# Opening of a fused FNet and gated-SwiGLU kernel: first x block in halves, high parts first, some splits and gate sums moved into later items

## The chip, the cores and the metric

The kernel runs on one core of one Trainium2 chip. The metric is device time in microseconds of one execution, median of several runs. A core has TensorE for matrix products, VectorE, ScalarE and GpSimd for elementwise work, SyncE (SP), and 16 DMA engines; each engine works through its own instruction stream in order, and streams wait for each other by semaphores.

## The reference

With x of 2048 x 512, fp32, the output is `g * a + (1 - g) * b`:

```
g = sigmoid((x * gate_w).sum(-1, keepdims=True))
a = re(DFT_seq) @ (x @ re(DFT_hid).T) - im(DFT_seq) @ (x @ im(DFT_hid).T)
b = (silu(x @ w1) * (x @ w3)) @ w2        # w1, w3: 512 x 1376, w2: 1376 x 512
```

The Fourier matrices come as inputs. All products are fp32.

## The kernel before, in words

**High and low parts.** An fp32 product is made from three products of a reduced type: high x high, high x low, low x high. `split` makes the parts: `high` (L108) is a ScalarE copy that rounds, `low` (L111) a VectorE subtraction of source and high part. `mm3` (L119) issues the three products of 128x128 weights with 512 columns.

**Strassen-Winograd.** Each large product is cut into 2 x 2 blocks and done with seven block products instead of eight. Of x there are the blocks B11, B12, B21, B22 and the differences T1 = B12 - B11, T2 = B22 - T1, T3 = B22 - B12 and T4 = B21 - T2; every one of the seven that are used (`OPS`) is split into the tile `xo`. Of a weight chunk (128 columns of w1 and of w3) three raw blocks, split into `wa` (places 0, 1 and 2, the last is A22), and four sums `wu` (L248 to L251), split into `wb`, are used. Weights arrive raw in `ws` tiles, four buffers in turn, so a load of chunk w + 4 waits until everything has read chunk w.

**The first stage.** The work on w1 and w3 goes in items, one per weight chunk and half of x (chunk 0 to 8 with half 0 first). Item 0 is done plainly, with eight block products (`plain`), because its forms are ready first: C00, C10, C01 and C11, each from two block products. Items 1 to 3 have their first two products, X (`first1`) and Y (`first2`), ahead of time. ScalarE copies X into `s1`; VectorE adds Y to it, the gate sum (L293); `gate1` is the Silu of that (L297). Before the items, this opening is ordered by a scheduler of the tile framework; from item 1 on the order is as written.

**An item**, `gate_up(n)`: X gets two sums' product (wb 1 with T2) and is copied (L356); then the list `early`; then the bank Z is begun (wb 2 with T3) and copied by ScalarE into `u4` (L359); then the sums of the next weights, the first product X of item n + 3 and the high part of the next wb; X gets wb 0 with T1 and VectorE adds it to `u4` (L367); the low part of the next wb; then the list `mid`; Z goes on accumulating in its bank with A22 and T4, and VectorE adds it and multiplies by the gate (L372, L373); the next-but-three weights are split; Y of item n + 3 and its gate sum; last, X gets wb 3 with B22, a Silu (L384) and a product (L388). Functions that are put into `early`, `mid` and `at_end` for an item run at these places; they fetch and split the second half of x, fetch and store other weights.

**Loads.** All loads are issued by SP in order, at first: the first block of chunk 0, B11, the other three blocks of chunk 0, B21, B12, chunk 1, B22, chunks 2 to 4. `load_xo` issues a block of x. Eleven small warm-up products (L398) run on TensorE until B11 is there. Stores of `wb` (L263) and of results (L322) are issued by GpSimd.

The later stages (Fourier products in blocks, w2, the output) are not touched by the change.

Of the kernel before, what the change touches and what calls it, by code (L numbers as in the profile page):

```python
# [7 lines left out]
F32 = mybir.dt.float32  # L8
# [4 lines left out]
P = 128  # L13
# [19 lines left out]
def fnet_swiglu_gate_kernel(  # L33
# [20 lines left out]
    nc = tc.nc  # L54

    def pool(name, bufs, side, space=None):
        kw = {} if space is None else {"space": space}
        cm = tc.tile_pool(name=name, bufs=bufs, side=side, reuse_waits="tile", **kw)
        return cm, cm.__enter__()
# [11 lines left out]
    wu_cm, wup = pool("wu", 1, "right")  # L71
# [8 lines left out]
    def bank(k, name):  # L80
        return psum.tile([P, 512], F32, tag=f"ps{k}", name=name)
# [14 lines left out]
    def wide(name):  # L96
        return take(F4, [P, 1024], F32, name)
# [4 lines left out]
    def free(*tiles):  # L102
        for t in tiles:
            _, places, at = HELD.pop(id(t))
            places.append(at)

    def high(hi, src):
        nc.scalar.activation(hi, src, AF.Copy)  # L108

    def low(hi, lo, src):  # L110
        nc.vector.tensor_sub(lo, src, hi.bitcast(F32))  # L111

    def split(hi, lo, src):
        high(hi, src)
        low(hi, lo, src)

    def mm3(ps, ah, al, bh, bl, first, last, chain=False):
        for n, (u, v) in enumerate(((ah, bh), (ah, bl), (al, bh))):
            nc.tensor.matmul(ps, u, v, start=first and n == 0, stop=last and n == 2,  # L119
                             skip_group_check=chain)  # L120
# [13 lines left out]
    def flat(ap):  # L134
        return ap.rearrange("p a n -> p (a n)")
# [53 lines left out]
    XO, ST = {}, {}  # L189
    XRAW = ("B12", "B11", "B21", "B22")  # L190

    def flat_x(ap):
        return ap.rearrange("p q n -> p (q n)")

    def load_xo(g, k):

        if g not in XO:
            XO[g] = (xo1 if g else xo0).tile([P, 2, 7, 2, 512], F32R, tag="xo", name=f"xo{g}")
        ST[g, k] = wide(f"xs{g}_{k}")
        nc.sync.dma_start(ST[g, k], xt[g, XRAW.index(k)])  # L200

    OPS = ("B11", "B21", "B22", "T1", "T2", "T3", "T4")
    SUMS = {"T1": ("B12", "B11"), "T2": ("B22", "T1"), "T3": ("B22", "B12"), "T4": ("B21", "T2")}
# [5 lines left out]
    def xo_parts(g, k):  # L209
        o = XO[g][:, :, OPS.index(k)]  # L210
        return flat_x(o[:, 0]), flat_x(o[:, 1]), ST[g, k]

    def split_xo(g, k):
        split(*xo_parts(g, k))

    WS, WA, WB = {}, {}, {}

    def back(w):
        return w >= NC and SETS[w] > 0
# [13 lines left out]
    def wa_parts(w, lo, hi):  # L233
        return (*(flat(WA[w][:, h, lo:hi]) for h in range(2)), flat(WS[w][:, lo:hi]))

    def prep_wa(w, lo=0, hi=3):

        if lo == 0:
            WA[w] = wap.tile([P, 2, 3, 256], F32R, tag="wa", name=f"wa{w}")
        split(*wa_parts(w, lo, hi))  # L240

    WU = {}

    def sums_wb(w):

        r = WS.pop(w)
        u = WU[w] = wup.tile([P, 4, 256], F32, tag="wu", name=f"wu{w}")
        nc.vector.tensor_add(u[:, 0], r[:, 3], r[:, 2])  # L248
        nc.vector.tensor_sub(u[:, 1], u[:, 0], r[:, 0])
        nc.vector.tensor_sub(u[:, 2], r[:, 0], r[:, 3])  # L250
        nc.vector.tensor_sub(u[:, 3], r[:, 1], u[:, 1])  # L251

    def wb_parts(w):
        return flat(WB[w][:, 0]), flat(WB[w][:, 1]), flat(WU[w])
# [15 lines left out]
    def prod(ps, n, wi, xi, start, chain=False):  # L270
        w = WSET[n]
        w, wi = (WA[w], wi) if wi < 3 else (WB[w], wi - 3)
        x = XO[ITEMS[n][1]]
        for q in range(2):
            sl = slice(q * P, (q + 1) * P)
            mm3(ps, w[:, 0, wi, sl], w[:, 1, wi, sl], x[:, 0, xi, q, :], x[:, 1, xi, q, :],
                start and q == 0, q == 1, chain)
# [9 lines left out]

    def first2(n):

        y = bank(4 + n % 2, f"Y{n}")  # L290
        prod(y, n, 1, 1, True)
        s1 = G[n][1]
        nc.vector.tensor_add(s1, s1, y)  # L293
        put_score(n, 0, s1)

    def gate1(n):
        nc.scalar.activation(G[n][1], G[n][1], AF.Silu)  # L297
# [28 lines left out]
    early, mid, at_end = {}, {}, {}  # L326
# [5 lines left out]
    def gate_up(n):  # L332
        last = NI - 1
        x, s1 = G.pop(n)
        z = bank(6 + n % 2, f"Z{n}")
        if n == last - 1:

            u2, g1 = (s1p.tile([P, 512], F32, tag="s1", name=f"{k}_{n}") for k in ("u2", "g1"))
        else:
            h = hp.tile([P, 1024], F32, tag="h", name=f"h{n}")  # L340
            u2, g1 = h[:, :512], h[:, 512:]
        u4 = u4p.tile([P, 512], F32, tag="u4", name=f"u4_{n}")
        nw = WSET[n + 1] if n < last else 0
        if nw in WB or nw == 0:
            nw = None
        elif back(nw):
            load_wb(nw)
            nw = None
        wa = WSET[n + LOOK + 1] if n + LOOK < last else 0
        if wa in WA or wa == 0:  # L350
            wa = None
        else:
            load_w(wa, 0, 3 if back(wa) else 4)

        prod(x, n, 4, 4, False, True)
        nc.scalar.activation(u2, x, AF.Copy)  # L356
        run(early, n)
        prod(z, n, 5, 5, True, True)
        nc.scalar.activation(u4, z, AF.Copy)  # L359
        if nw is not None:  # L360
            sums_wb(nw)
        if n + LOOK <= last:
            first1(n + LOOK)
        if nw is not None:
            high_wb(nw)
        prod(x, n, 3, 3, False, True)
        nc.vector.tensor_add(u4, u4, x)  # L367
        if nw is not None:
            low_wb(nw)
        run(mid, n)  # L370
        prod(z, n, 2, 6, False, True)
        nc.vector.tensor_add(u2, u2, z)  # L372
        nc.vector.tensor_mul(u2, s1, u2)  # L373
        store_h(n, 0, u2)
        if wa is not None:
            WA[wa] = wap.tile([P, 2, 3, 256], F32R, tag="wa", name=f"wa{wa}")
            parts_a = wa_parts(wa, 0, 3)
            high(parts_a[0], parts_a[2])
        if n + LOOK <= last:
            first2(n + LOOK)  # L380
        if wa is not None:
            low(*parts_a)
        prod(x, n, 6, 2, False, True)
        nc.scalar.activation(g1, x, AF.Silu)  # L384
        put_score(n, 1, x)
        if n + LOOK <= last:
            gate1(n + LOOK)
        nc.vector.tensor_mul(g1, g1, u4)  # L388
        store_h(n, 1, g1)
        run(at_end, n)  # L390
# [10 lines left out]
    def plain(b12, a21):  # L401

        c = {}

        def half(i, j, w, x, start):
            if start:
                c[i, j] = bank((0, 4, 6, 7)[2 * i + j], f"C{i}{j}")
            for r in range(2):
                sl = slice(r * P, (r + 1) * P)
                mm3(c[i, j], w(0, sl), w(1, sl), x(r, 0), x(r, 1), start and r == 0,  # L410
                    not start and r == 1)

        def wa(k):
            return lambda h, sl: WA[0][:, h, k, sl]

        def xb(k):
            return lambda q, h: XO[0][:, h, k, q, :]

        w21 = lambda h, sl: a21[:, h, sl]
        x12 = lambda q, h: b12[:, h, q * 512 : (q + 1) * 512]  # L420
        s1 = s1p.tile([P, 512], F32, tag="s1", name="s1_0")
        g1 = u4p.tile([P, 512], F32, tag="u4", name="g1_0")
        h = hp.tile([P, 1024], F32, tag="h", name="h0")
        yield half(0, 0, wa(0), xb(0), True)
        yield half(1, 0, w21, xb(0), True)
        half(0, 0, wa(1), xb(1), False)
        nc.scalar.activation(s1, c[0, 0], AF.Silu)
        yield half(1, 0, wa(2), xb(1), False)
        nc.vector.tensor_mul(h[:, :512], s1, c[1, 0])
        store_h(0, 0, h[:, :512])  # L430
        half(0, 1, wa(0), x12, True)
        yield half(1, 1, w21, x12, True)
        half(0, 1, wa(1), xb(2), False)
        nc.scalar.activation(g1, c[0, 1], AF.Silu)
        half(1, 1, wa(2), xb(2), False)
        nc.vector.tensor_mul(h[:, 512:], g1, c[1, 1])
        yield store_h(0, 1, h[:, 512:])
# [31 lines left out]
    gate1(1)  # L469
    sum_xo(0, "T1", hp.tile([P, 1024], F32, tag="h", name="t1"))  # L470
    sum_xo(0, "T2", ST[0, "B11"])
    prep_wa(2)
    first1(2)
    first2(2)
    gate1(2)
    split_xo(0, "T2")
    prep_wb(1)
    sum_xo(0, "T3", ST[0, "B12"])
    split_xo(0, "T3")
    prep_wa(3)  # L480
    first1(3)
    first2(3)
    gate1(3)
    split_xo(0, "T1")
    prep_wa(4)
    sum_xo(0, "T4", ST[0, "B21"])
    split_xo(0, "T4")
    free(*(ST[0, b] for b in ("B11", "B21", "B12", "B22")))

    def do(work, n, f, *a):  # L490
        work.setdefault(n, []).append(lambda: f(*a))


    for k in ("B11", "B21", "B12", "B22"):
# [79 lines left out]
    n = NI - 1 - LOOK  # L574
# [335 lines left out]
    for i, (src, sp, p) in enumerate(late):  # L910
        blk, b = 1 + i // 2, i % 2
        n = (17, 24)[b]
# [11 lines left out]
    for p in range(KD):  # L924
        early = p < NG - NP2
# [71 lines left out]
```

## Time and profile before

| | |
|---|---|
| median of 3 runs | 712.57 us (712.29 to 712.75) |
| profiled execution | 712.41 us, span 710.6 us |
| TensorE, VectorE, ScalarE busy | 99%, 85%, 52% of the span |
| products of the first kernel item start | 5.63 us |
| from 15 us to 30 us | TensorE and VectorE both busy 4.98 to 5.00 of each 5 us |

A row of a timeline holds its start and length in us, the engine, the line, the operation, the tiles written and read, shapes and count; in brackets the idle time before it and who ended it. Equal instructions that follow each other are merged. A product shows a length of some 0.39 us, but the next starts 0.23 us after it: the products overlap. Tile names stand without their numbers: `C` is a bank of item 0, `X`, `Y`, `Z` those of the later items, `s` the gate sums and their Silu, `u` the tile `u4` and `h` the results.

### The profile page before, as it was taken

The numbers are of one execution on the slowest core, as the hardware profiler recorded it, in microseconds if no ns is written. First come the engines' busy times: TensorE is split into PE (matmuls) and PEld (weight loads), VectorE is DVE, ScalarE is ACT, GpSimd is POOL, SyncE is SP. The second block draws the span as 40 slices with busy tenths as digits, with TensorE's granted clock in tenths as the row PEclk, the third lists the DMA queues.
The fourth block names the chain that finished last, engine by engine and source line by source line (L and its number), as shares of the span: only waits on it lengthen the run. The fifth ranks groups of instructions, "written<-read, shape, count | busy, mean of one in ns | idle before, by whom it ended". The sixth has DMA issues, their size and how long they took to land.

```text
span 710.6 us, 8590 instructions
## 1 busy us (share of the span) xinstructions
PE 704.8 (99%) x3089; PEld 578.7 (81%) x3089; DVE 602.4 (85%) x731; ACT 369.0 (52%) x477; POOL 65.7 (9%) x120
## 2 busy tenths in 40 slices
PE   9999999999999999999999999999999999999997
PEld 5888888888888887888888888888888888888886
DVE  6979988787679989886999599969997896898985
ACT  6665555655445755454554553544445355445451
POOL 0011111121110000000110001100110000000000
PEclk9999999999999999999999999999999999999999
DMA  7585546489997496712496228915999971773932
GB/s 280 190 300 209 211 191 254 183 308 353 420 413 267 159 323 226 302 60 89 159 350 276 89 99 318 367 40 199 371 419 416 362 264 63 296 278 140 322 119 89
DMA packets 45691, 173.59 MB, mean 244 GB/s; under 512 B 5328, under 2 KB 5456, under 8 KB 41808
## 3 DMA queue, kind: packets, MB, share of 16 engines
q1 hardware_dynamic: 32464, 118.50, 45.2%
q0 software_dynamic: 12896, 54.02, 19.7%
q8 instruction: 24, 0.39, 0.2%
q10 hardware_dynamic: 288, 0.52, 0.2%
q14 instruction: 19, 0.16, 0.1%
HBM read 115.87 MB, written 57.16 MB: 243 GB/s over the span
## 4 chain that ended last, share of the span: by engine, by line
PE 90%; DVE 4%; DMA 3%; ACT 1%; issue 1%; SPq 0%; POOL 0%; ACTq 0%; DVEq 0%; POOLq 0%
PE P L119 61%; PE X L119 16%; PE Z L119 8%; PE Y L119 4%; DVE zo L111 2%; DMA B<-cc 1%; PE C L119 1%; DVE B L653 1%; DMA xs_B<-xt 1%; ACT zo L108 1%; DMA gate<-gsp 0%; DVE a L111 0%; ACT L730 0%; DVE xo L111 0%; DVE B L656 0%
## 5 line engine op out<-in xcount | busy, mean ns | idle before, releaser
L119 PE MATMUL P<-zo,a 128*128 128x512 f32 x1344 | 306.0, 390 | 0.5 <-DVE zo L111 0.5
L119 PEld LDWEIGHTS P<-zo,a 128*128 128x128 f32 x1344 | 251.8, 188 | 54.5 <-DVE zo L111 2.4
L108 ACT ACTIVATE zo<-B 128x1024 fp32r<-128x1024 f32 (+1 forms) x182 | 189.1, 1045 | 186.2 <-PE P L119 95.9
L111 DVE TENSOR_TENSOR zo<-B,zo 128x1024 fp32r<-128x1024 f32 (+1 forms) x182 | 218.0, 1206 | 50.0 <-ACT zo L108 49.2
L119 PE MATMUL P<-zo,H 128*128 128x512 f32 x468 | 106.2, 389 | 0.0
L119 PEld LDWEIGHTS P<-zo,H 128*128 128x128 f32 x468 | 87.8, 188 | 18.2
L653 DVE TENSOR_TENSOR B<-B,B 128x1024 f32<-128x1024 f32 (+1 forms) x78 | 93.2, 1195 | 0.1
L119 PE MATMUL X<-xo,wb 128*128 128x512 f32 x378 | 92.7, 389 | 0.0
L119 PEld LDWEIGHTS X<-xo,wb 128*128 128x128 f32 x378 | 70.9, 188 | 14.7
L119 PE MATMUL P<-zo,Y 128*128 128x512 f32 x336 | 76.3, 389 | 0.0
L119 PEld LDWEIGHTS P<-zo,Y 128*128 128x128 f32 x336 | 63.1, 188 | 13.1
L322 POOL DMA_DIRECT2D hsp<-h x42 | 23.0, 548 | 127.0 <-DVE h L373 75.5
L119 PE MATMUL X<-xo,wa 128*128 128x512 f32 x126 | 32.3, 389 | 0.0
L119 PE MATMUL Z<-xo,wa 128*128 128x512 f32 x126 | 32.3, 390 | 0.0
L119 PE MATMUL Y<-xo,wa 128*128 128x512 f32 x126 | 32.1, 389 | 0.0
L119 PE MATMUL Z<-xo,wb 128*128 128x512 f32 x126 | 32.1, 389 | 0.0
L870 ACT ACTIVATE zu<-P 128x512 f32<-128x512 f32 x32 | 19.0, 597 | 20.3 <-PE P L119 20.3
L367 DVE TENSOR_TENSOR u<-u,X 128x512 f32<-128x512 f32 x21 | 14.4, 687 | 17.6 <-PE X L119 15.3
L656 DVE TENSOR_TENSOR B<-B,B 128x1024 f32<-128x1024 f32 x24 | 29.3, 1219 | 0.0
L119 PEld LDWEIGHTS Z<-xo,wa 128*128 128x128 f32 x126 | 23.6, 188 | 5.3 <-DVE xo L111 0.4
L119 PEld LDWEIGHTS Y<-xo,wa 128*128 128x128 f32 x126 | 23.6, 188 | 4.9
L119 PEld LDWEIGHTS X<-xo,wa 128*128 128x128 f32 x126 | 23.6, 188 | 4.9
(134 smaller groups left out, 553.8 us busy)
## 6 DMA issues: line engine op xcount, KB each, us to landing
B<-cc SPq DMA_DIRECT2D x64, 512.0 KB, 6.7
hsp<-h POOLq DMA_DIRECT2D x42, 256.0 KB, 3.7
B<-hsp SPq DMA_DIRECT2D x20, 512.0 KB, 10.4
wbsp<-wb POOLq DMA_DIRECT2D x8, 1024.0 KB, 4.2
wb<-wbsp SPq DMA_DIRECT2D x8, 1024.0 KB, 7.8
B<-zsp SPq DMA_DIRECT2D x16, 512.0 KB, 8.2
H<-w2sp SPq DMA_DIRECT2D x6, 1024.0 KB, 8.9
ws<-w SPq DMA_DIRECT2D x11, 512.0 KB, 6.9
```

What stands on the lines that cost most here:

```text
L108: nc.scalar.activation(hi, src, AF.Copy)
L111: nc.vector.tensor_sub(lo, src, hi.bitcast(F32))
L119: nc.tensor.matmul(ps, u, v, start=first and n == 0, stop=last and n == 2, skip_group_check=chain)
L322: nc.gpsimd.dma_start(hsp[g, b + k, j // 2, :, j % 2 * 512 : (j % 2 + 1) * 512], h)
L367: nc.vector.tensor_add(u4, u4, x)
L653: nc.vector.tensor_add(t, t, RAW[blk, b, q][:, :n])
L656: nc.vector.tensor_sub(t, RAW[blk, "B12", q], t)
L870: nc.scalar.activation(U[name][:, r], ps[r], AF.Copy)
```

## The change

The first block of x that is loaded, B11 of half 0, comes in two loads of 512 columns. In item 0 the three kinds of products stand in another order: for both rows, high x high and low x high, which need only x's high part, then high x low for both. In the opening, weights 2 to 4 are split in places 0 and 1 only; A22 (place 2) of weights 2, 3 and 4 is split in `mid` of items 1, 2 and 3. Y of items 2 and 3 is multiplied in the opening as before (`prod2`), but the gate sum and Silu of item 2 stand in `early` and those of item 3 in `mid` of item 1. T4 of half 0 is split in `early` of item 1, with the first two sums of weights 2 between its high and low part; the other two sums stay where all four were. The raw blocks of x are given back there too.

```diff
@@ load_xo @@
-        nc.sync.dma_start(ST[g, k], xt[g, XRAW.index(k)])
+        n = 512 if not g and k == "B11" else 1024
+        for i in range(0, 1024, n):
+            nc.sync.dma_start(ST[g, k][:, i : i + n], xt[g, XRAW.index(k), :, i : i + n])
@@ sums_wb @@
-    def sums_wb(w):
-        r = WS.pop(w)
-        u = WU[w] = wup.tile([P, 4, 256], F32, tag="wu", name=f"wu{w}")
-        nc.vector.tensor_add(u[:, 0], r[:, 3], r[:, 2])
-        nc.vector.tensor_sub(u[:, 1], u[:, 0], r[:, 0])
-        nc.vector.tensor_sub(u[:, 2], r[:, 0], r[:, 3])
-        nc.vector.tensor_sub(u[:, 3], r[:, 1], u[:, 1])
+    def sums_wb(w, lo=0, hi=4):
+        r = WS[w]
+        if w not in WU:
+            WU[w] = wup.tile([P, 4, 256], F32, tag="wu", name=f"wu{w}")
+        u = WU[w]
+        for i, (f, a, b) in enumerate(((nc.vector.tensor_add, r[:, 3], r[:, 2]),
+                                       (nc.vector.tensor_sub, u[:, 0], r[:, 0]),
+                                       (nc.vector.tensor_sub, r[:, 0], r[:, 3]),
+                                       (nc.vector.tensor_sub, r[:, 1], u[:, 1]))):
+            if lo <= i < hi:
+                f(u[:, i], a, b)
@@ first2 @@
     def first2(n):
+        sum_g(n, prod2(n))
+
+    def prod2(n):
         y = bank(4 + n % 2, f"Y{n}")
         prod(y, n, 1, 1, True)
+        return y
+
+    def sum_g(n, y):
         s1 = G[n][1]
         nc.vector.tensor_add(s1, s1, y)
         put_score(n, 0, s1)
@@ gate_up @@
         if nw is not None:
-            sums_wb(nw)
+            sums_wb(nw, 2 if nw in WU else 0)
@@ plain, half @@
-            for r in range(2):
-                sl = slice(r * P, (r + 1) * P)
-                mm3(c[i, j], w(0, sl), w(1, sl), x(r, 0), x(r, 1), start and r == 0,
-                    not start and r == 1)
+            v = [(slice(r * P, (r + 1) * P), r) for r in range(2)]
+            v = ([(w(h, sl), x(r, 0)) for sl, r in v for h in range(2)]
+                 + [(w(0, sl), x(r, 1)) for sl, r in v])
+            for n, (a, b) in enumerate(v):
+                nc.tensor.matmul(c[i, j], a, b, start=start and n == 0,
+                                 stop=not start and n == len(v) - 1)
@@ the opening @@
-    prep_wa(2)
+    prep_wa(2, 0, 2)
     first1(2)
-    first2(2)
-    gate1(2)
+    y2 = prod2(2)
     split_xo(0, "T2")
     prep_wb(1)
     sum_xo(0, "T3", ST[0, "B12"])
     split_xo(0, "T3")
-    prep_wa(3)
+    prep_wa(3, 0, 2)
     first1(3)
-    first2(3)
-    gate1(3)
+    y3 = prod2(3)
     split_xo(0, "T1")
-    prep_wa(4)
+    prep_wa(4, 0, 2)
     sum_xo(0, "T4", ST[0, "B21"])
-    split_xo(0, "T4")
-    free(*(ST[0, b] for b in ("B11", "B21", "B12", "B22")))
...
+    do(early, 1, lambda: high(*xo_parts(0, "T4")[::2]))
+    do(early, 1, sums_wb, 2, 0, 2)
+    do(early, 1, lambda: low(*xo_parts(0, "T4")))
+    do(early, 1, free, *(ST[0, b] for b in ("B11", "B21", "B12", "B22")))
+    for n, work, y in ((2, early, y2), (3, mid, y3)):
+        do(work, 1, sum_g, n, y)
+        do(work, 1, gate1, n)
+    for w in (2, 3, 4):
+        do(mid, w - 1, lambda v=wa_parts(w, 2, 3): split(*v))
```

## The prediction

> **What bounds the kernel now.** I read the page first, for the engine that sets the span, then the waits of TensorE over the whole run, then the timelines of the first 62 us engine by engine, because the edit touches nothing later.
>
> ```profile
> span 710.6 us, 8590 instructions
> PE 704.8 (99%) x3089; PEld 578.7 (81%) x3089; DVE 602.4 (85%) x731; ACT 369.0 (52%) x477; POOL 65.7 (9%) x120
> PE 90%; DVE 4%; DMA 3%; ACT 1%; issue 1%; SPq 0%; POOL 0%; ACTq 0%; DVEq 0%; POOLq 0%
> PE P L119 <- DVE zo L111: 0.5, 1, 0.5
> ```
>
> TensorE is busy 99% of the span, and the waits after 60 us hold a single one of its own, 0.5 us. The number of products is unchanged, so time can only be won or lost where TensorE waits. Those places, by its timeline (start, length, line, tiles, count; the last two rows are weight loads):
>
> ```profile
> 5.00 1.06 PE L398 MATMUL wps<-warm 128*128 128x512 bf16 x2
> 5.63 2.21 PE L119 MATMUL C<-xo,wa 128*128 128x512 f32 x6
> 7.68 1.52 PE L119 MATMUL C<-xo,a 128*128 128x512 f32 x6
> 9.04 0.61 PE L119 MATMUL C<-xo,wa 128*128 128x512 f32 x2
> 10.01 2.60 PE L119 MATMUL C<-xo,wa 128*128 128x512 f32 x10 [0.36 <-DVE xo L111]
> 12.45 1.53 PE L119 MATMUL C<-b,wa 128*128 128x512 f32 x6
> ...
> 19.25 1.52 PE L119 MATMUL Y<-xo,wa 128*128 128x512 f32 x6
> 20.61 1.52 PE L119 MATMUL X<-xo,wa 128*128 128x512 f32 x6
> ...
> 31.49 1.82 PE L119 MATMUL Z<-xo,wa 128*128 128x512 f32 x6
> 33.15 1.53 PE L119 MATMUL Y<-xo,wa 128*128 128x512 f32 x6
> ...
> 38.60 1.52 PE L119 MATMUL X<-xo,wa 128*128 128x512 f32 x6
> ```
> ```profile
> 5.63 0.29 PEld L119 LDWEIGHTS C<-xo,wa 128*128 128x128 f32 x1 [0.48 <-ACT xo L108]
> 6.36 1.05 PEld L119 LDWEIGHTS C<-xo,wa 128*128 128x128 f32 x5 [0.44 <-DVE xo L111]
> ```
>
> Six products fill 1.36 us (19.25 to 20.61), 0.227 each. Against that pitch the first six (5.63 to 7.68) lose 0.69; the two at 9.04 lose 0.52 and the ten at 10.01 another 0.17, waiting for the low part of x's B21; and the six at 31.49 take 1.66 to the next row, 0.30 too long, waiting for the low part of T4. All else up to 38.60 runs at pitch. So at most about 1.7 us, plus something of the first 5.63, can be won here: 0.2% of this kernel, which is also about what its measurement can tell from no change, is 1.43 us.
>
> The engines that feed it, and the loads:
>
> ```profile
> 4.95 1.15 ACT L108 ACTIVATE xo<-xs_B 128x512 fp32r<-128x512 f32 x2 [1.40 <-DMA xs_B<-xt]
> 6.09 0.42 ACT L108 ACTIVATE a<-ws 128x256 fp32r<-128x256 f32 x1
> 7.64 1.06 ACT L108 ACTIVATE xo<-xs_B 128x1024 fp32r<-128x1024 f32 x1 [0.61 <-DMA xs_B<-xt]
> ...
> 29.03 0.60 ACT L359 ACTIVATE u<-Z 128x512 f32<-128x512 f32 x1 [0.82 <-PE Z L119]
> 29.52 1.05 ACT L108 ACTIVATE xo<-xs_B 128x1024 fp32r<-128x1024 f32 x1
> 30.47 0.62 ACT L297 ACTIVATE s<-s 128x512 f32<-128x512 f32 x1
> 30.99 0.59 ACT L285 ACTIVATE s<-X 128x512 f32<-128x512 f32 x1
> ...
> 42.88 0.85 ACT L108 ACTIVATE wa<-ws 128x768 fp32r<-128x768 f32 x1 [0.17 <-PE Z L119]
> ```
> ```profile
> 8.73 1.23 DVE L111 TENSOR_TENSOR xo<-xs_B,xo 128x1024 fp32r<-128x1024 f32 x1 [0.89 <-ACT xo L108]
> ...
> 20.01 0.42 DVE L251 TENSOR_TENSOR wu<-ws,wu 128x256 f32<-128x256 f32 x1
> 20.35 1.22 DVE L207 TENSOR_TENSOR xs_B<-xs_B,xs_B 128x1024 f32<-128x1024 f32 x1
> 21.49 0.68 DVE L293 TENSOR_TENSOR s<-s,Y 128x512 f32<-128x512 f32 x1
> 22.08 1.22 DVE L111 TENSOR_TENSOR wb<-wu,wb 128x1024 fp32r<-128x1024 f32 x1
> ...
> 30.61 1.22 DVE L111 TENSOR_TENSOR xo<-xs_B,xo 128x1024 fp32r<-128x1024 f32 x1 [0.17 <-ACT xo L108]
> ...
> 36.69 0.95 DVE L111 TENSOR_TENSOR wa<-ws,wa 128x768 fp32r<-128x768 f32 x1
> ...
> 41.99 0.69 DVE L367 TENSOR_TENSOR u<-u,X 128x512 f32<-128x512 f32 x1 [2.28 <-ACT wb L108]
> ...
> 51.11 0.69 DVE L367 TENSOR_TENSOR u<-u,X 128x512 f32<-128x512 f32 x1 [1.29 <-PE X L119]
> ```
> ```profile
> 1.75:2.25 0.50, 0.50 (x3) 0.15 (x1) 0.00 (x0) 0.49 (x2) 0.00 (x0) 1.00 0.46 156
> 4.00:5.00 1.00, 1.00 (x3) 0.30 (x2) 0.01 (x1) 0.05 (x1) 0.00 (x0) 1.00 0.99 373
> 25.00:30.00 5.00, 5.00 (x24) 4.14 (x23) 4.98 (x7) 2.80 (x5) 0.00 (x0) 1.00 0.45 184
> ```
> ```profile
> 1.18 0.42 SPq L200 DMA_DIRECT2D xs_B<-xt  x1
> 1.65 0.42 SPq L224 DMA_DIRECT2D ws<-w  x1
> 33.24 27.33 SPq L224 DMA_DIRECT2D ws<-w  x4
> ```
>
> In the windows (PE, PEld, DVE, ACT, POOL busy, clock, DMA share, GB/s) VectorE works 4.98 of 5 us from 25 to 30: it is full just ahead of the T4 wait, and that is what the second half of the edit unloads. One operation occupies VectorE by the starts of neighbours: 0.34 us for 256 columns (20.01 to 20.35), 1.14 for 1024, 0.59 for 512. ScalarE: 0.49 for a 512-column copy, 0.95 for 1024, 0.52 for a Silu. A hand-off between the two costs about 0.03 (the T4 high part, 29.52 + 1.05, to its low part at 30.61: 0.04), to TensorE 0.05 (8.73 + 1.23 to 10.01).
>
> **The front.** The warm-up products start 0.43 apart (two rows' worth in 5.00 + 1.06, the last taking 0.63), the last at 5.43, so the next product cannot start before 5.86 at that rate. The whole B11 had landed by 4.95, so its first half lands between 3.1 (the load ahead of it) and 4.95; at 373 GB/s I get 4.95 - 0.70 = 4.25. Its high part is then ready near 4.9, well before 5.86: the halves alone buy nothing at the start, and the second half, whose high part is ready near 5.6, is not late either. What the new order of the six products buys is that the second one no longer waits for x's low part (6.36). The first goes at the slow rate (5.86 to 6.29), the second partly (to 6.61; before, five products from 6.36 to 7.68 take 1.32 instead of 1.13, so the full rate began about there), four more end at 7.52. Before: 7.68. Six with A21 then end at 8.88.
>
> Then B21. Its high part is ready at 7.64 + 1.06 = 8.70, its low part at 9.96. Four high products of C00 and two of C10 now come first, and the low part is wanted only at 8.88 + 1.36 = 10.24. Nothing waits, and the twelve end at 11.60, before at 12.45: 0.85 us won. Price of the extra load instruction: SP spends 0.47 on it (1.18 to 1.65), and all loads behind it are issued that much later. They were not waiting for SP (the DMA engines are 99% busy from 4 to 5), so I take 0. If it all reached B21, its high part would come at 9.17, 0.29 too late: gain 0.56. If the low-rate start ended sooner, gain up to 1.1. So 0.85, from 0.56 to 1.1.
>
> From there to the products of X2 nothing waits: 19.76 instead of 20.61.
>
> **The moved work.** Two gate sums, three A22 splits and T4's split leave the opening; VectorE gets them back in items 1 to 3, where it idles (2.28 us ahead of 41.99, 1.29 ahead of 51.11). The work is not cheaper (a 768-column low part is now 512 and 256 columns, 0.59 + 0.34 for 0.87); it is moved. Where it lands is the point. In item 1 it goes into the slot "early", which is written before ScalarE's copy of Z1, and TensorE's products of weights A22 and T4 go on accumulating in Z1's bank, so they must wait for that copy (L359, at 29.03 before). In the changed program ScalarE's order is T4's high part, Silu of chunk 2, copy of Z1, and that Silu waits for chunk 2's gate sum, which VectorE does after T4's low part.
>
> In VectorE's new order the chain starts at chunk 1's gate sum, which waits for Y1. Y1's last product starts at 19.53 and ends 0.39 later: 19.95. Then 0.59 + 0.34 (a weight sum) + 1.14 (T3) + 0.59 (weights 3) + 3 x 1.14 (wb1, T3, T1) + 0.59 (weights 4) brings T4's difference to 26.62. It ends at 27.84; high part 27.87 to 28.93; low part from 28.96, next operation at 30.10; gate sum to 30.78; Silu from 30.81, Z1's copy 0.52 later, 31.33 to 31.93; TensorE at 31.98. TensorE, meanwhile, runs X2, Y2, X3, Y3, X1, Z1, X4, X1 from 19.76, 48 products, to 30.64. So it waits 1.34 us, more than the 0.30 that T4 cost before. The first products after a wait lose a little more (the ten at 10.01 lose 0.17, once started); I take 0.11. Y4 starts at 31.98 + 1.36 + 0.11 = 33.45; before 33.15. The 0.85 is spent, and 0.30 more.
>
> Bounds: the wait cannot be shorter than 0 nor, if Silu and sum both stood behind one more 1024-column operation, longer than 2.5. I take 1.34, since every duration in it is a row above.
>
> Second place: weights 5, wanted by X5's third product, two pitches after X5 starts. X5 now stands at 33.45 + 4 x 1.36 = 38.89, third product 39.34. On ScalarE behind Z1's copy: copy of X4 from 31.82, high part of wb2 from 32.31 to 33.37. VectorE: its low part from 33.40, chunk 3's gate sum 34.54 to 35.22. ScalarE: Silu 35.25, then the high part of A22 of weights 2 (0.42, as at 6.09) 35.77 to 36.19. VectorE: its low part 36.22, sum 36.56, product 37.27 (it needs the sum), gate sum 4 37.86, weights 5 from 38.45 to 39.40 (36.69 before). TensorE could go on at 39.45: 0.11 of wait, 0.11 of slow restart. Before, that work had been done at 37.64 for a product at 39.05. Third product: 39.56 against 39.05.
>
> Loads of weights 6 to 8 now wait for the A22 splits: weights 6 would be issued at 36.6 instead of about 33.2 (last SP row) and is wanted by ScalarE a little after the 42.88 of before; 6 us of slack hide it. Later items have the same order on every engine, only shifted.
>
> **Sum** on the profiled 710.6 us span (run 712.41): -0.85 - 0.30 (the old T4 wait) + 1.45 + 0.22 = +0.52, 712.9; the median of the runs, 712.57, is 0.16 above that run: 713.1.
>
> **Rivals.**
> *The copy of Z1 is not held up* (the Silu's input is ready early, or the copy runs ahead of it). For it: VectorE has 0.87 + 0.59 + 0.59 us less to do before T4. Against it: the copy stands behind the Silu, and the Silu behind T4's low part. Then -0.85 - 0.30 and nothing back: 711.4. The Trainium skill, "TensorE: Matmul & The Clock Gate", table at its head, calls ScalarE's queue strictly first in, first out; by that rule this rival is excluded; no row above shows an instruction passing another. 0.12.
>
> *The halves land slowly, and all loads behind them* (slower than before). Rows of 1 KB moved at 156 GB/s (1.75 to 2.25), rows of 3 and 4 KB at 373. The halves have rows of 2 KB. At 156 the two take 3.36 us instead of 1.41, B21's high part is 1.95 late, of which 0.18 is slack: 1.77 lost, 714.9. At the mean, 265, 0.57 late, 0.39 lost: 713.5. It passes 714.0, slower by more than 0.2%, once the loads come 1.1 us late, below about 210 GB/s for the halves. Against it: at 1.75 the loads had just begun. The Trainium skill, "DMA: Bandwidth & Descriptors", section "Bandwidth", advises transfers of 1 MiB and up and gives 138 GB/s at 64 KB and 341 at 1 MB; an estimate of mine between them for 256 KB, 240 GB/s, would make it 713.7. 0.18.
>
> *VectorE falls further behind in item 1*: weights 5 has no slack left, so each microsecond there is one of TensorE's. With the 2.5 us bound at Z1 in place of 1.34, 714.3; from 0.9 us more than forecast it decides. For it: three hand-offs to and from ScalarE instead of one. Against it: each costs 0.03 or 0.04. 0.12.
>
> **Numbers.** My forecast, a change too small to tell, +0.5 us, has 0.58. It and the gentle half of the second rival lie within 711.15 to 714.0: same 0.73. Slower 0.20: the hard half of the second, most of the third. Faster 0.07: 711.4 and a little luck. The range, 711.8 to 714.4, reaches past the third rival and leaves out the first and the far end of the second.
>
> **What would show it.** Right: first product of A21 near 7.5 and of B12 near 11.6, no wait at 10; then a wait of 1.2 to 1.5 us of TensorE for ScalarE's copy of Z near 30.6, ScalarE idle near 29 to 31 for the gate sum; a short wait near 39. Wrong: no wait at 30.6 (first rival); ScalarE's B21 split after 7.9 (second); a wait above 0.5 us near 39 (third). It would also fail if a stall after 60 us moved.

## The result: slower by about a quarter of a per cent

The changed kernel takes 714.35 us (median of 10 runs, 713.64 to 714.82) against 712.40 (10 runs, 712.03 to 712.78); the ratio is 1.0026, with a 95% interval of 1.0018 to 1.0035. That is +1.9 us where +0.5 was forecast. The time lies within the forecast range (711.8 to 714.4), at its upper end, but above 714.0, up to which the prediction counts the change as the same: what came is the outcome "slower", which it gave 0.20. The profiled execution took 714.21 us, span 712.4 (before 712.41 and 710.6), so the two traces show 1.8 us of the difference.

The busy times of the page and the waits of TensorE over the whole run, changed kernel (who waited, its line, for whom: us in total, times, longest):

```profile
PE 704.8 (99%) x3089; PEld 578.3 (81%) x3089; DVE 603.3 (85%) x734; ACT 369.1 (52%) x480; POOL 65.9 (9%) x120
```
```profile
PE Z L119 <- ACT u L371: 1.3, 1, 1.3
PE wps L410 <- DVE warm L407: 1.2, 1, 1.2
PE C L425 <- ACT xo L108: 0.8, 1, 0.8
PE P L119 <- DVE zo L111: 0.7, 2, 0.5
```

TensorE's busy time is the same to the tenth; two waits of TensorE in the first stage are new, 1.3 us for ScalarE's copy of Z and 0.8 us for ScalarE's split of x. Where they stand, by the timeline of TensorE, after:

```profile
5.21 1.75 PE L425 MATMUL C<-xo,wa 128*128 128x512 f32 x6
6.87 1.89 PE L425 MATMUL C<-xo,a 128*128 128x512 f32 x6
9.54 3.03 PE L425 MATMUL C<-xo,wa 128*128 128x512 f32 x12 [0.78 <-ACT xo L108]
12.41 1.52 PE L425 MATMUL C<-b,wa 128*128 128x512 f32 x6
...
27.44 1.52 PE L119 MATMUL Z<-xo,wb 128*128 128x512 f32 x6
...
30.16 1.52 PE L119 MATMUL X<-xo,wb 128*128 128x512 f32 x6
32.93 1.66 PE L119 MATMUL Z<-xo,wa 128*128 128x512 f32 x6 [1.25 <-ACT u L371]
34.43 1.53 PE L119 MATMUL Y<-xo,wa 128*128 128x512 f32 x6
...
39.87 1.77 PE L119 MATMUL X<-xo,wa 128*128 128x512 f32 x6
41.48 1.53 PE L119 MATMUL X<-xo,wb 128*128 128x512 f32 x6
```

Read against the rows of before, start for start. The products of A21 start at 6.87 instead of 7.68, but those of B21 at 9.54, after a gap; by B12 (12.41 against 12.45) nothing is left of the lead. Z at 32.93 comes 2.77 us after the row ahead of it, where 1.36 would do: 1.41 lost, and 0.14 more in the slow start. Y4 is at 34.43 against 33.15, +1.28. X5 takes 1.61 instead of 1.36, +0.25, which makes +1.53. The rest, some 0.3, comes much later: TensorE's wait for VectorE near 270 us is 0.7 in all instead of 0.5. Sum +1.8. What is lost at that place differs in all the profiles, by starts from 0.36 less to 0.32 more than before, also between kernels that differ only in the first 40 us.

The two engines that it waits for, after:

```profile
4.14 0.63 ACT L108 ACTIVATE xo<-xs_B 128x512 fp32r<-128x512 f32 x1 [0.59 <-DMA xs_B<-xt]
5.03 0.63 ACT L108 ACTIVATE xo<-xs_B 128x512 fp32r<-128x512 f32 x1 [0.25 <-DMA xs_B<-xt]
...
8.43 1.06 ACT L108 ACTIVATE xo<-xs_B 128x1024 fp32r<-128x1024 f32 x1 [1.09 <-DMA xs_B<-xt]
...
28.81 1.06 ACT L108 ACTIVATE xo<-xs_B 128x1024 fp32r<-128x1024 f32 x1 [0.58 <-DVE xs_B L209]
31.76 0.63 ACT L309 ACTIVATE s<-s 128x512 f32<-128x512 f32 x1 [1.89 <-DVE s L305]
32.30 0.58 ACT L371 ACTIVATE u<-Z 128x512 f32<-128x512 f32 x1
```
```profile
29.91 1.23 DVE L111 TENSOR_TENSOR xo<-xs_B,xo 128x1024 fp32r<-128x1024 f32 x1 [0.33 <-ACT xo L108]
31.05 0.68 DVE L305 TENSOR_TENSOR s<-s,Y 128x512 f32<-128x512 f32 x1
```

The chain from T4 to Z is seen link by link: T4's high part ends at 29.87, its low part starts at 29.91, the gate sum of chunk 2 follows at 31.05, ScalarE idles 1.89 us until it has that sum, does the Silu at 31.76, and only then the copy of Z1, at 32.30. Z1's products, from 27.44, had long ended, and TensorE has been waiting for the copy since 31.52. The first half of B11 did land early (4.14), and the second (5.03) about when the whole had before (4.95); but B21 is split from 8.43, before from 7.64.

### The profile page after: what moved, and what is told of

It reads as the page before. It is cut to its first block, busy times and chain, and to the rows that moved or that the text cites. A ratio compares the mean times of both kernels' runs of the same rounds, so it can differ in the third digit from the quotient of the medians.

```text
span 712.4 us, 8595 instructions
## 1 busy us (share of the span) xinstructions
PE 704.8 (99%) x3089; PEld 578.3 (81%) x3089; DVE 603.3 (85%) x734; ACT 369.1 (52%) x480; POOL 65.9 (9%) x120
## 4 chain that ended last, share of the span: by engine, by line
PE 88%; DVE 6%; DMA 3%; ACT 2%; issue 1%; SPq 0%; POOL 0%; ACTq 0%; DVEq 0%; POOLq 0%
PE P L119 61%; PE X L119 15%; PE Z L119 8%; PE Y L119 3%; DVE zo L111 2%; DMA B<-cc 1%; PE C L425 1%; DVE B L675 1%; DMA xs_B<-xt 1%; DVE xo L111 1%; ACT zo L108 1%; DMA gate<-gsp 0%; ACT xo L108 0%; DVE a L111 0%; DVE xs_B L209 0%
```

## The experiments

All times are medians, and each ratio is against the kernel before on the same chip (712.30 to 712.38 us). A row of ScalarE's split of a block that waited for the DMA tells by its start when the block had landed.

**Only the new order of item 0's products.**

```diff
@@ plain, half @@ (in the kernel before)
-            for r in range(2):
-                mm3(c[i, j], w(0, sl), w(1, sl), x(r, 0), x(r, 1), ...)
+            v = ([(w(h, sl), x(r, 0)) for sl, r in v for h in range(2)]
+                 + [(w(0, sl), x(r, 1)) for sl, r in v])
```

> Only the new order of item 0's products; B11 in one load, nothing moved. Theory A (the gain of the front is real, but VectorE has to keep up): B21's wait at 10 us goes (0.85 us earlier at B12, about 11.6 instead of 12.45), but VectorE is full from 12 to 31 us, so TensorE runs into it again ahead of 35 us, at weights 4 or T4, and gives back at least the 0.85: 712.4 to 714. Theory B (the front's gain reaches the end, the loss of the changed kernel lies in the halves alone): 711.5.

Measured: 714.05 us, ratio 1.0025 (1.0015 to 1.0035). TensorE in this run:

```profile
11.80 1.52 PE L413 MATMUL C<-b,wa 128*128 128x512 f32 x6
...
32.00 0.49 PE L119 MATMUL Z<-xo,wa 128*128 128x512 f32 x1 [0.25 <-ACT xo L108]
33.74 1.43 PE L119 MATMUL Z<-xo,wa 128*128 128x512 f32 x5 [1.24 <-DVE xo L111]
35.00 1.55 PE L119 MATMUL Y<-xo,wa 128*128 128x512 f32 x6
```

The front's gain is there (B12 at 11.80 instead of 12.45), and is more than lost again by Y4, at 35.00 instead of 33.15. The time is at the upper end of what theory A allows. Not all of that is VectorE being full: with the new order the scheduler of the opening also places T4's low part later, behind the last two weight sums and the addition to `u4`; it starts at 32.46, before at 30.61. Theory B, that the front's gain reaches the end, is out; how much of the loss the scheduler's order is, this run does not part.

**Only the moved gate sums and splits.** The changed kernel with the old order in `half` and one load of B11.

```diff
-            v = ([(w(h, sl), x(r, 0)) for sl, r in v for h in range(2)]
-                 + [(w(0, sl), x(r, 1)) for sl, r in v])
+            for r in range(2):
+                mm3(c[i, j], w(0, sl), w(1, sl), x(r, 0), x(r, 1), ...)
-        n = 512 if not g and k == "B11" else 1024
+        nc.sync.dma_start(ST[g, k], xt[g, XRAW.index(k)])
```

> Only the moved gate sums, A22 and T4 splits; old order of item 0, B11 in one load. Theory A (Z1's copy behind the Silu of chunk 2, and weights 5 behind chunk 3's Silu, cost): TensorE waits about 0.7 to 1.3 us for ScalarE's copy of Z1 near 31.5 and 0.2 to 0.4 at X5 near 39.5; 713.2 to 713.9. Theory B (the loss is in the halves): 712.1, the 0.3 us of the old T4 wait won.

Measured: 713.22 us, ratio 1.0014 (1.0005 to 1.0023).

```profile
32.00 1.66 PE L119 MATMUL Z<-xo,wa 128*128 128x512 f32 x6 [0.56 <-ACT u L369]
...
38.95 1.76 PE L119 MATMUL X<-xo,wa 128*128 128x512 f32 x6
```

Both waits are there without any change of the front, so the moved work alone makes the kernel slower, by 0.9 us. The one for Z1's copy is shorter than expected, 0.56 (0.73 by starts).

**Only the two half loads.**

```diff
-        nc.sync.dma_start(ST[g, k], xt[g, XRAW.index(k)])
+        n = 512 if not g and k == "B11" else 1024
+        for i in range(0, 1024, n):
+            nc.sync.dma_start(ST[g, k][:, i : i + n], xt[g, XRAW.index(k), :, i : i + n])
```

> Only the two half loads of B11; old order, nothing moved. If the halves delay the loads behind them, ScalarE's split of B21 starts near 8.4 us instead of 7.64, and TensorE's wait for B21's low part grows by about 0.8: 713.2. If the late B21 of the changed kernel's profile was chance, the split starts near 7.7 and the time is 712.4.

Measured: 713.21 us, ratio 1.0012 (1.0003 to 1.0021). ScalarE and TensorE:

```profile
8.39 1.06 ACT L108 ACTIVATE xo<-xs_B 128x1024 fp32r<-128x1024 f32 x1 [1.25 <-DMA xs_B<-xt]
```
```profile
7.13 1.55 PE L119 MATMUL C<-xo,a 128*128 128x512 f32 x6
9.50 0.73 PE L119 MATMUL C<-xo,wa 128*128 128x512 f32 x2 [0.82 <-ACT xo L108]
10.76 2.54 PE L119 MATMUL C<-xo,wa 128*128 128x512 f32 x10 [0.53 <-DVE xo L111]
13.13 1.52 PE L119 MATMUL C<-b,wa 128*128 128x512 f32 x6
```

B21 at 8.39, as in the changed kernel. The late load is no chance. The halves do bring TensorE to A21 earlier, at 7.13 instead of 7.68, but it then waits for B21: B12 is 0.68 late, and the kernel 0.9 us slower.

**The changed kernel with B11 in one load.** The last hunk of the second diff above.

> The changed kernel with B11 in one load. If the halves cost what their profile shows (B21 0.8 us late), B12's products start near 11.6 instead of 12.41, but TensorE then meets the same wait for Z1's copy, longer by what was won if VectorE sets the time of T4: 713.2 to 713.7. If the halves cost nothing, 714.35 as the changed kernel.

Measured: 713.23 us, ratio 1.0010 (1.0001 to 1.0019).

```profile
11.86 1.52 PE L423 MATMUL C<-b,wa 128*128 128x512 f32 x6
...
32.35 1.66 PE L119 MATMUL Z<-xo,wa 128*128 128x512 f32 x6 [1.25 <-ACT u L369]
33.84 1.53 PE L119 MATMUL Y<-xo,wa 128*128 128x512 f32 x6
```

The halves cost 1.1 us of the 1.9. And set beside the run with the moved work alone (713.22), the new order is worth nothing here: B12 starts 0.37 us earlier than in that run (12.23 there), but the wait for Z1's copy is 1.25 instead of 0.56, and Y4 starts at 33.84 against 33.49. VectorE does not follow TensorE's lead: it starts T4's difference at 26.98, in that run at 26.20.

**The Silu of chunk 2 out of the way of Z1's copy.** From here on, one load of B11.

```diff
     for n, work, y in ((2, early, y2), (3, mid, y3)):
         do(work, 1, sum_g, n, y)
-        do(work, 1, gate1, n)
+        do(mid, 1, gate1, n)
```

> As the changed kernel with B11 in one load, and the Silu of chunk 2 moved from the slot ahead of Z1's copy to the later slot of item 1 (its gate sum stays). If the Silu in front of Z1's copy is what TensorE waits for, the wait near 31 us (1.3 us in the run without halves) is gone, and X5 is met 1 us earlier than weights 5 can be ready, so the wait near 38.5 grows from 0.2 to about 0.7: 712.0. If something else holds Z1 (T4's low part itself), a wait above 0.5 us stays there: 712.8 or more.

Measured: 712.41 us against 712.30, ratio 1.0005 (0.9996 to 1.0014): no difference from the kernel before.

```profile
30.72 1.52 PE L119 MATMUL Z<-xo,wa 128*128 128x512 f32 x6
32.08 1.52 PE L119 MATMUL Y<-xo,wa 128*128 128x512 f32 x6
...
38.83 1.21 PE L119 MATMUL X<-xo,wa 128*128 128x512 f32 x4 [0.70 <-DVE wa L111]
```

The wait at Z is gone, with nothing changed but the place of one Silu; the one at X5 has grown to 0.70, the size expected. The time is 0.4 us above the 712.0 expected; by starts X5 loses 1.00 (39.88 - 37.52 - 1.36).

**Both Silus behind A22's split.**

```diff
-    for n, work, y in ((2, early, y2), (3, mid, y3)):
-        do(work, 1, sum_g, n, y)
-        do(work, 1, gate1, n)
+    do(early, 1, sum_g, 2, y2)
+    do(mid, 1, sum_g, 3, y3)
     for w in (2, 3, 4):
         do(mid, w - 1, lambda v=wa_parts(w, 2, 3): split(*v))
+    for n in (2, 3):
+        do(mid, 1, gate1, n)
```

> As the run before, and in the later slot of item 1 A22 of weights 2 is split before the two Silus, so that VectorE does not wait for the Silu of chunk 3 ahead of weights 5. If that hand-off is the second cost, no wait is left in the first 60 us: about 1.1 us less than the kernel before, 711.2 to 711.5. If weights 5 are late because VectorE has too much to do, the wait near 38.5 stays: 712.0.

Measured: 711.13 us (710.71 to 711.87), ratio 0.9984 (0.9975 to 0.9992). All waits of TensorE in this run:

```profile
PE wps L408 <- DVE warm L405: 1.2, 1, 1.2
PE P L119 <- DVE zo L111: 0.5, 1, 0.5
```

Only the start and the old wait near 270 us are left, and the kernel is faster than both. VectorE's low part of A22 of weights 2, which stands ahead of weights 5 in its queue, in the run before and in this one:

```profile
35.55 0.43 DVE L111 TENSOR_TENSOR wa<-ws,wa 128x256 fp32r<-128x256 f32 x1 [1.00 <-ACT wa L108]
```
```profile
34.80 0.42 DVE L111 TENSOR_TENSOR wa<-ws,wa 128x256 fp32r<-128x256 f32 x1
```

VectorE had the same work to do; what made weights 5 late was the 1.00 us in which it waited for ScalarE's high part, which stood behind the Silu of chunk 3.

**Two loads of B11 by partitions**, in the kernel before: 64 rows of 4 KB each.

```diff
-        nc.sync.dma_start(ST[g, k], xt[g, XRAW.index(k)])
+        n = P // 2 if not g and k == "B11" else P
+        for i in range(0, P, n):
+            nc.sync.dma_start(ST[g, k][i : i + n], xt[g, XRAW.index(k), i : i + n])
```

> The kernel before with B11 in two loads by partitions: 64 rows of 4 KB each, instead of 128 rows of 2 KB. If a load more in the queue delays those behind it, B21's split starts near 8.4 us as with the column halves, and the time is 713.2. If the rows of 2 KB do, it starts near 7.7: 712.4.

Measured: 713.84 us, ratio 1.0020 (1.0011 to 1.0029). ScalarE's split of B21:

```profile
9.15 1.06 ACT L108 ACTIVATE xo<-xs_B 128x1024 fp32r<-128x1024 f32 x1 [1.21 <-DMA xs_B<-xt]
```

With full 4 KB rows it is later still, 9.15, so the delay does not need short rows. Here B11 itself is late too (split from 5.69, in the kernel before from 4.95); halves of 64 partitions may have a cost of their own, which this run does not part.

**Ten warm-up products instead of 11**, on the run with the gates last (`WARM = 10`).

> The run with the gates last, with 10 warm-up products instead of 11. If the last warm-up product is what the first product waits for, it starts up to 0.3 us earlier, near 5.6, and the front ends about 0.2 us earlier: 711.0 to 711.3. If B11's landing or B21 sets the front, nothing changes.

Measured: 711.26 us, ratio 0.9988 (0.9979 to 0.9996). The first product's row and ScalarE's split of B11 in this profile, then in that with 11:

```profile
5.64 1.49 PE L423 MATMUL C<-xo,wa 128*128 128x512 f32 x5
4.96 1.15 ACT L108 ACTIVATE xo<-xs_B 128x512 fp32r<-128x512 f32 x2 [1.39 <-DMA xs_B<-xt]
```
```profile
5.96 1.82 PE L423 MATMUL C<-xo,wa 128*128 128x512 f32 x5
5.28 1.15 ACT L108 ACTIVATE xo<-xs_B 128x512 fp32r<-128x512 f32 x2 [1.69 <-DMA xs_B<-xt]
```

It starts 0.3 us earlier, but not because of the warm-up. In both profiles it comes 0.68 after the split of B11 starts, and it comes 0.68 or 0.69 after it in every profile with B11 in one load and 11 warm-up products, too: 4.95 and 5.63 in the kernel before, 5.42 and 6.10 in the changed kernel with B11 in one load. B11's landing sets this start, as the second theory has it, and varies by half a microsecond from profile to profile. The time shows no difference either: the median is no lower, and the 0.2 us expected is smaller than the spread of the runs (0.6 us and more).

**The halves put back into the kernel with the gates last**, first with both issued by SP, then with the second issued by ScalarE (`q = nc.scalar if i else nc.sync`).

> The run with the gates last, with the two half loads of B11 put back, both issued by SP. B21's split should start near 8.4 again (7.56 there) and TensorE wait for its high part about 0.6 us near 9, with no other wait before 60 us: 711.13 + 0.6 = 711.7. If the halves only hurt together with the other waits: 711.1.

> The same, but the second half is issued by ScalarE's own queue instead of SP's. If one load more in SP's queue is what delays the loads behind it, B21's split starts near 7.6 and the time is that of the whole load, 711.1. If one load more on the DMA engines is, whoever issues it, B21's split starts near 8.4 and the time is 711.7.

Measured: 712.28 us, ratio 0.9997 (0.9988 to 1.0006), and 712.69 us, ratio 1.0001 (0.9992 to 1.0010); the run without halves had 0.9984 (0.9975 to 0.9992). ScalarE's split of B21 and the wait, SP first:

```profile
8.48 1.06 ACT L108 ACTIVATE xo<-xs_B 128x1024 fp32r<-128x1024 f32 x1 [1.04 <-DMA xs_B<-xt]
```
```profile
PE C L425 <- ACT xo L108: 0.6, 1, 0.6
```

And with ScalarE as the issuer:

```profile
8.85 1.06 ACT L108 ACTIVATE xo<-xs_B 128x1024 fp32r<-128x1024 f32 x1 [0.32 <-DMA xs_B<-xt]
```

So the halves cost 0.9 us (by the ratios) to 1.15 us (by the medians) also where nothing else is in the way, more than the 0.6 expected; and issuing the second one from ScalarE does not take the cost away. The profiles show only half of it (B12 at 12.48 instead of 11.94): that of the run without halves is the slowest of its eleven runs. The effect shows in what the DMA engines move (windows: last two columns DMA share and GB/s), in the kernel before and then in the changed kernel:

```profile
5.00:6.00 1.00, 1.00 (x4) 0.44 (x2) 0.39 (x1) 1.00 (x2) 0.00 (x0) 1.00 0.95 366
6.00:7.00 1.00, 1.00 (x5) 0.55 (x4) 1.00 (x3) 1.00 (x3) 0.00 (x0) 1.00 1.02 406
```
```profile
4.00:5.00 1.00, 1.00 (x4) 0.33 (x3) 0.20 (x2) 0.63 (x1) 0.00 (x0) 1.00 0.91 268
5.00:6.00 1.00, 1.00 (x6) 0.74 (x5) 0.81 (x2) 0.63 (x1) 0.00 (x0) 1.00 0.76 246
6.00:7.00 1.00, 1.00 (x6) 0.57 (x4) 0.54 (x2) 0.60 (x2) 0.00 (x0) 1.00 0.83 295
```

For three microseconds they move 268, 246 and 295 GB/s where they moved 373, 366 and 406, though SP had issued B21 and B12, which they carry, by 3.5 us. Why one transfer more thins the stream for that long stays open: neither short rows nor SP as the only issuer are needed for it, and no view here shows the inside of the queues.

## Why the prediction was right and wrong, step by step

- *The wait for Z1's copy*: right in place, cause and size (1.34 forecast; 1.25 in the profile, 1.41 with what the restart adds by starts). TensorE and the copy both came about 0.9 us later than forecast (31.52 against 30.64, 32.30 against 31.33), because both follow from Y1, so the difference between them held. The run that moves one Silu removes the wait and so shows the cause. ScalarE did not let the copy pass the waiting Silu: it idled 1.89 us with Z complete. This agrees with the strict order that the Trainium skill, "TensorE: Matmul & The Clock Gate", table at its head, gives for ScalarE's queue. The first rival is out.
- *Weights 5*: right in place and cause. 0.22 forecast, 0.25 measured; the low part that ends it started at 39.44 (38.45 forecast, the whole item being later).
- *The old T4 wait gone*, *loads of weights 6 to 8 hidden*: right. Z goes on at 32.93 behind the copy, T4's low part having ended at 31.14; and though SP issues those loads only from 37.63 on (36.6 forecast, 33.24 before), all rows of TensorE from 41.48 to 62 run at pitch.
- *The front*: wrong, and here the forecast failed. The step is "Price of the extra load instruction ... I take 0", bounded at the 0.47 us that SP spends on it. B21 came 0.79 late (8.43 against 7.64), outside that bound, while the DMA engines moved less than before; the prediction had named a split after 7.9 as the sign of its second rival. Of 0.85 forecast as won, 0.04 was (12.41 against 12.45). By the runs, the halves cost 0.9 to 1.15 us in each of three settings. Without them the change costs 0.7 (by the ratio) to 0.9 us (by the medians), not far from the +0.5 forecast; with them, 1.9. I bounded the extra load by what its issue takes, and did not put the second rival's price into the sum.
- *The start of the front* was misread too. The sum holds the first product back to 5.86, for the last warm-up product, and concludes that the halves buy nothing there. But before, it starts at 5.63, only 0.20 after the last warm-up product's start and 0.68 after that of B11's split, and with the halves it starts at 5.21, A21 at 6.87 (7.52 forecast). The halves bought what the prediction denied them, and the late B21 took it.
- *The range* holds the time by 0.05 us, and by luck: its upper end was drawn to reach past the third rival's 714.3, a longer wait at Z1, which did not come.
- *The second rival* had the place and the size, not the cause. It has the halves themselves land slowly, for their rows of 2 KB; they landed about on time (splits from 4.14 and 5.03), and 4 KB rows in two transfers are no better. The estimate made there from the Trainium skill, "DMA: Bandwidth & Descriptors", section "Bandwidth" (240 GB/s for 256 KB, 0.77 us late), is by size of transfer, not of row. The table behind it is of transfers issued by GpSimd; here SP issues them. That 0.79 was measured is luck, since the time was lost behind the halves and not in them. The rule to batch agrees in direction: B21 is split from 8.39 to 9.15 in all five profiles that have B11 in two loads, and from 7.44 to 7.64 in the other seven.
- *The new order's 0.85* was right as a mechanism (no wait for B21 at 10 us in the runs with one load; B12 at 11.62 to 11.94 instead of 12.45, so 0.5 to 0.8), but it was booked as a gain by itself. Alone it made the kernel 1.7 us slower, and with the moved work it was eaten whole by Z1's wait, because T4's chain on VectorE does not come earlier with it. Why it does not is open: B11 landed later in that profile (5.42 against 4.98), and the scheduler of the opening orders VectorE differently; the runs do not part the two.
- *Nothing after 60 us*: 0.3 us more was lost near 270 us, not foreseen. It is no more than that place varies from profile to profile.

## What to carry to other kernels

A step put into an earlier slot is to be read on every in-order engine that it touches: one Silu, itself 0.6 us, ahead of a copy that frees a bank for TensorE cost 1.3 us because its input came from another engine's full queue. A transfer split in two to start earlier was paid for here by the transfers behind it; while the DMA engines are busy all the time, price it by the landing of the next ones and not by its issue. And where TensorE is the bound and its feeders are nearly full, a gain at the front is only worth what the next wait leaves of it.

## What the runs showed that was not expected

The warm-up products and the first products of item 0 do not run at one rate from run to run. Eleven equal warm-up products, before and after:

```profile
1.19 4.87 PE L398 MATMUL wps<-warm 128*128 128x512 bf16 x11 [1.19 <-DVE warm L395]
```
```profile
1.19 4.37 PE L410 MATMUL wps<-warm 128*128 128x512 bf16 x11 [1.19 <-DVE warm L407]
```

Before, all of them start about 0.43 us apart; after, the last ones start closer. So the full rate came while they ran, where before it came only behind them. The Trainium skill, "TensorE: Matmul & The Clock Gate", Part 1, says that the clock is released by a window of activity that runs freely, whatever the kernel's start. A change of rate that comes at another time in each profile fits that, but the granted clock reads 1.00 in every window of the first microseconds of both profiles, so no run here shows that it is the clock. With B11 in halves of columns, both issued by SP, the first product follows right behind the warm-up, and the start of item 0 moves with it: 5.01, 5.21 and 5.50 us for warm-ups of 4.17, 4.37 and 4.88 us. There it hides behind B21's landing, so it decides nothing in the changed kernel.
